# Attention, a feed-forward block and a gated convolution: both heads' scores of a pair from separate halves of the array

## The chip, the cores and the metric

The kernel runs on one core of one Trainium2 chip. The metric is the device time of one execution in microseconds; the time before is the median of three executions. Engines: TensorE (PE; its weight loads are shown apart as PEld), VectorE (DVE), ScalarE (ACT), GpSimd (POOL), SyncE (SP), from whose queue all loads and stores are issued.

## The reference, cut to what matters

```python
# q, k, v: (8, 8, 576, 64): 8 batches, 8 heads, 576 positions, 64 wide
scores = (q @ k.T) / 8.0
scores = where(row // 64 >= col // 64, scores, -1e9)       # causal by blocks of 64
attn = exp(scores - rowmax); attn = attn / (rowsum + 1e-9)
x = heads side by side of (attn @ v)                       # (8, 576, 512)
u = x + ((x.T @ U) @ V).T                                  # rank 32 over positions
u = u + relu(u @ w_ch1) @ w_ch2                            # 512 -> 2048 -> 512
gate = sigmoid(causal convolution of u with 5 taps, per channel)
out = (gate * (u @ w_val)) @ w_out
```

## The kernel before, in words

There are 64 heads, handled in pairs: queries and keys of a pair are loaded together as 128 rows (64 of each head) by 576 columns, and VectorE transposes them in 32 x 32 blocks (`prep_t`, lines 348 to 366). One call of `tick(n, ...)` (line 723) is one step of a software pipeline: it computes the scores of head n and, two heads behind, the product with v of head e = n - 2 (`emit_pv`), with the exponents of head e + 1 between them (`emit_est`); `mixing` puts in the rank-32 mixing of finished pairs. `tick` is a generator; each `yield` is a point at which other work may be put in.

Scores come in two forms. Heads 0 to 17 (n < NQ = 18) have queries on the rows: `emit_q_bank` (line 420) makes four PSUM banks of scores per head in plain float32, 1856 columns in all. Both heads' transposed queries are the stationary operand on all 128 rows, and the moving operand is a copy of the head's keys that holds zeros on the other head's 64 rows (the tiles ks and qs of the list kz, zeroed in `setup_att`). VectorE masks a block, takes the row maxima from PSUM and ScalarE writes the exponents from PSUM; TensorE transposes those later (`emit_q_turn`).

Heads 18 to 63 have keys on the rows: `emit_s_piece` (line 389) computes the scores in four pieces of 512, 320, 448 and 320 columns (1600 in all; the first is made of stretches of 64, 192 and 256), each in its own PSUM bank. The operands are rounded parts in the one-pass format float32r, made by `prep_qk` (line 368): ScalarE rounds q once and k twice (three casts of 64 x 576, helper line 93), GpSimd clears half of a tile (line 380) and subtracts for the two remainders kl and qs (helper line 99). Two 128-row matmuls per stretch of columns (lines 397 and 398) then give high by high plus high by low, and low by high. ScalarE copies each piece to a buffer (line 402), GpSimd sets the masked corners (`emit_corners`, line 475), VectorE finds the column maxima (`emit_max_a`, `emit_max_b` and `emit_max_c`, lines 488 to 522, with small copies between partitions at 508 to 518) and subtracts them (`emit_sub`, line 525, five instructions a head at line 528); ScalarE takes the exponents in place (line 550) and rounds them, VectorE takes the remainders el.

What sets the order. TensorE runs in the order in which the code is written. The other engines' instructions are ordered beforehand by a planner that works with the dependences and its own estimates, and each engine then runs its queue in that order. Up to about 127 us only attention runs (with the splitting of the feed-forward weights on ScalarE, VectorE and GpSimd). From then on the loop at line 1083 goes over 9 groups of 512 positions with 16 slices of the hidden layer each: `emit_h1` makes a slice (12 matmuls into a PSUM tile h, read by ScalarE as hh and by VectorE as the remainder hl, lines 869 and 870), `emit_o` adds the slice before it to four accumulators (12 matmuls, line 887). At four places of each slice `gap()` takes the next step or steps of the attention from `tick`, at a pace that `aim` sets so that a batch of eight heads is done when its group is due; what is not done by then is run off before the next group starts. In this stage the accumulators hold four of the eight PSUM banks, and score tiles, h, and all tiles of attention share the other four (the pool of `ps_p`, tag a). Before it the scores have four banks of their own. From about 1085 us only the feed-forward block is left, and from about 1325 us the gated stage.

Of the kernel before, what the change touches and what calls it, by code (L numbers as in the profile page):

```python
# [22 lines left out]
def attn_moe_gate_kernel(ctx: ExitStack, tc: tile.TileContext, q, k, v, U, V, w1, w2, wval, convw, wout, out):  # L23
# [35 lines left out]
    QV = 10  # L59
    KV = 0  # L60
# [138 lines left out]
    st_p = rpool("stp", 1)  # L199
    s_p = rpool("sp", 2)  # L200
# [103 lines left out]
    def setup_att():  # L304
        for t in vstk:
            pool.memset(t[:, :, D:P], 1.0)
            pool.memset(t[0:D, NK - 1, :], 0.0)
        for a in range(2):
            for t in kz:
                pool.memset(t[a][own[1 - a]], 0.0)  # L310
# [29 lines left out]
    def pads(nm, dtype):  # L340
        return [st_p.tile([P, S], dtype, tag=f"{nm}{a}", name=f"{nm}{a}") for a in range(2)]

    kz = [pads(nm, F32) for nm in ("ks", "qs")]
    ks, qs = [], []
    kl = st_p.tile([P, S], F32R, name="kl")
    qkt = {}

    def prep_t(pn):
        if pn >= B * NP:
            return  # L350
        t = raw.pop(pn)
        if 2 * pn < NQ:
            tq = rot("tk" if pn % 2 else "tq", 1)
            z = kz[pn % 2]
            for rows in own if pn == 0 else (slice(0, P),):
                vec.transpose(tq[rows], t["q"][rows])
                for a in range(2):
                    if pn or rows == own[a]:
                        vec.transpose(z[a][own[a]], t["k"][own[a]])
            qkt[pn] = (tq, z)  # L360
        else:
            tq, tk = rot("tq", 1), rot("tk", 1)
            vec.transpose(tq, t["q"])
            vec.transpose(tk, t["k"])
            qkt[pn] = (tq, tk)
        load_qk(pn + 1)

    def prep_qk(n):
        if n >= B * H or n < NQ:
            return  # L370
        if not ks:
            ks.extend(pads("ks", F32R))
            qs.extend(pads("qs", F32R))
        tq, tk = qkt[n // 2]
        a = n % 2
        me, ot = own[a], own[1 - a]
        hi_act(qs[a][me], tq[me])
        hi_act(ks[a][me], tk[me])
        hi_act(ks[a][ot], tk[me])
        pool.memset(f32(kl[ot]), 0.0)  # L380
        lo(vec if n < KV else pool, kl[me], tk[me], ks[a][me])
        lo(vec if n < QV else pool, qs[a][ot], tq[me], qs[a][me])

# [5 lines left out]
    def emit_s_piece(n, i):  # L389
        pr, a = divmod(n, 2)  # L390
# [781 lines left out]
```

## Time and profile before

| | |
|---|---|
| three executions | 1532.7 us median, 1532.04 to 1533.65 |
| the profiled execution | 1538.09 us, span in the profile 1536.3 us |
| TensorE busy | 1427.0 us, 93% of the span (weight loads 1151.1) |
| VectorE busy | 1146.3 us, 75% |
| ScalarE busy | 789.5 us, 51% |
| GpSimd busy | 516.1 us, 34% |
| DMA | 163.58 MB, 106 GB/s over the span |

A busy share is an average over stages with different limits, so the stretches have to be read by themselves. A matmul's recorded length includes its way through the array; how many follow each other in a time is read from their starts. One float32 matmul leaves two records (a weight load and a matmul each), a float32r matmul one. The granted clock is that of TensorE, 1.00 being 2.4 GHz; it has two levels, and the other is 1.2 GHz.

### The profile page before, as it was taken

Reading aid. Unit: us, or ns where it says so; the run is one execution under the profiler, and the core shown is the slowest. Engines: PE = TensorE matmul, PEld = TensorE weight load, DVE = VectorE, ACT = ScalarE, POOL = GpSimd, SP = SyncE. Lnnn points to the kernel's source line nnn. Section 1 sums busy time; section 2 is a strip of 40 time slices with the busy share of each in tenths; the row PEclk is TensorE's granted clock in tenths of the full one; section 3 lists DMA queues with packets and bytes.
Section 4 is the critical chain, followed back from the end, with each engine's and each line's share of the span. In section 5 each row is a group of like instructions: output and inputs, shape, how many; then the busy total and the mean of one; then the engine's idle time right before and its main releaser. Section 6 shows DMA issues by size and latency. Waiting matters only on the chain. (4 is left out here: it accounts for less than half of the span.)

```text
span 1536.3 us, 20391 instructions
## 1 busy us (share of the span) xinstructions
PE 1427.0 (93%) x6664; PEld 1151.1 (75%) x6664; DVE 1146.3 (75%) x2252; ACT 789.5 (51%) x1639; POOL 516.1 (34%) x587
## 2 busy tenths in 40 slices
PE   5897899979989998999899989989999999999999
PEld 2665677868767787777687778768888888778887
DVE  7887874659887888788888878887624427399991
ACT  4785565546565665666476556655512212243432
POOL 3133232333435333534443444335104210353410
PEclk8998999989999999999999999999999999999999
DMA  7555662224233333333323333232225543323221
GB/s 171 142 133 167 204 194 79 79 80 103 79 81 114 85 86 105 92 79 89 109 79 90 92 92 93 78 85 90 77 83 198 174 135 123 105 68 103 78 74 69
DMA packets 246291, 163.58 MB, mean 106 GB/s; under 512 B 197669, under 2 KB 212261, under 8 KB 246186
## 3 DMA queue, kind: packets, MB, share of 16 engines
q1 hardware_dynamic: 246186, 162.29, 36.6%
q8 instruction: 53, 0.87, 0.2%
q14 instruction: 52, 0.43, 0.1%
HBM read 134.98 MB, written 27.26 MB: 106 GB/s over the span
## 5 line engine op out<-in xcount | busy, mean ns | idle before, releaser
L887 PE MATMUL acc<-hh,w 128*128 128x512 f32 x1152 | 408.4, 405 | 10.2 <-ACT hh L869 10.2
L887 PEld LDWEIGHTS acc<-hh,w 128*128 128x128 f32 x1152 | 220.7, 192 | 57.7 <-ACT hh L869 12.8
L841 PE MATMUL h<-uh,w1hi 128*128 128x512 f32 x576 | 239.1, 415 | 9.9 <-DVE hl L870 6.3
L887 PE MATMUL acc<-hl,w 128*128 128x512 f32 x576 | 230.2, 400 | 5.9 <-DVE hl L870 5.9
L841 PE MATMUL h<-uh,w1lo 128*128 128x512 f32 x576 | 228.2, 396 | 0.0
L841 PE MATMUL h<-ul,w1hi 128*128 128x512 f32 x576 | 228.0, 396 | 0.0
L870 DVE SCALAR_TENSOR_TENSOR hl<-h,hh 128x512 fp32r<-128x512 f32 x144 | 98.2, 682 | 116.1 <-ACT hh L869 115.4
L869 ACT ACTIVATE hh<-h 128x512 fp32r<-128x512 f32 x144 | 85.8, 596 | 154.3 <-PE h L841 147.4
L550 ACT ACTIVATE s<-s 128x448 f32<-128x448 f32 x92 | 65.5, 712 | 150.0 <-DVE s L528 149.0
L841 PEld LDWEIGHTS h<-uh,w1hi 128*128 128x128 f32 x576 | 110.7, 192 | 35.8 <-DVE hl L870 8.2
L402 ACT COPY s<-pS 128x320 f32<-128x320 f32 (+2 forms) x184 | 89.8, 490 | 80.9 <-PE pS L398 77.2
L887 PEld LDWEIGHTS acc<-hl,w 128*128 128x128 f32 x576 | 110.5, 192 | 27.5 <-DVE hl L870 8.2
L841 PEld LDWEIGHTS h<-uh,w1lo 128*128 128x128 f32 x576 | 109.7, 190 | 24.8
L841 PEld LDWEIGHTS h<-ul,w1hi 128*128 128x128 f32 x576 | 110.7, 192 | 18.3 <-issue 1.4
L528 DVE TENSOR_TENSOR s<-s,mb 128x64 f32<-128x64 f32 (+4 forms) x230 | 123.0, 598 | 1.3
L962 DVE SCALAR_TENSOR_TENSOR gt<-yb,cw,gt 128x516 f32<-128x516 f32 (+1 forms) x144 | 116.5, 839 | 1.4
L99 POOL TENSOR_TENSOR vlo<-vstk,vhi 128x320 fp32r<-128x320 f32 x46 | 54.3, 1180 | 161.1 <-ACT vhi L93 148.1
L99 POOL TENSOR_TENSOR yl<-yb,yh 128x512 fp32r<-128x512 f32 (+7 forms) x64 | 67.7, 1091 | 96.9 <-ACT yh L93 96.8
L99 POOL TENSOR_TENSOR ul<-xt,uh 128x512 fp32r<-128x512 f32 (+7 forms) x64 | 53.2, 840 | 132.6 <-ACT uh L93 131.9
L397 PE MATMUL pS<-qs,ks 128*128 128x320 f32 (+4 forms) x276 | 80.4, 309 | 6.3 <-ACT lt L614 4.2
L398 PE MATMUL pS<-qs,kl 128*128 128x320 f32 (+4 forms) x276 | 82.4, 302 | 0.0
L99 DVE TENSOR_TENSOR el<-s,eh 128x448 fp32r<-128x448 f32 x92 | 76.7, 859 | 5.2 <-issue 4.6
(152 smaller groups left out, 3105.5 us busy)
## 6 DMA issues: line engine op xcount, KB each, us to landing
w<-w_s SPq DMA_DIRECT2D x144, 512.0 KB, 3.2
rawq<-in_q_dram SPq DMA_DIRECT2D x128, 72.0 KB, 2.4
rawk<-in_k_dram SPq DMA_DIRECT2D x128, 72.0 KB, 2.5
out_dram<-ot SPq DMA_DIRECT2D x35, 256.0 KB, 2.0
raw<-in_moe_w_ch_dram SPq DMA_DIRECT2D x64, 128.0 KB, 2.3
raw<-in_moe_w_ch_dram SPq DMA_DIRECT2D x16, 512.0 KB, 4.2
vstk<-in_v_dram SPq DMA_DIRECT2D x64, 128.0 KB, 2.6
w_s<-wo SPq DMA_DIRECT2D x16, 512.0 KB, 3.6
```

Of the source, the lines that this page charges most:

```text
L99: eng.tensor_tensor(o, i, f32(h), op=ALU.subtract)
L397: pe.matmul(ps[:, o:o + w], ks[a][:, kslice(j)], qs[a][:, a0:a1], start=True, stop=False)
L398: pe.matmul(ps[:, o:o + w], kl[:, kslice(j)], qs[a][:, a0:a1], start=False, stop=True)
L402: act.copy(stt[n][half_of[j]][:, d:d + o], ps[:, 0:o])
L528: noted(3, vec.tensor_tensor(sv(n, j), sv(n, j), mb[:, q0[j]:], op=ALU.subtract))
L550: act.activation(s, s, AF.Exp, scale=scale)
L841: pe.matmul(ps[:, 0:n], w[:, d, fs], x[:, d, 0:n], start=(d == 0 and i == 0), stop=(d == ND - 1 and i == 2))
L869: act.activation(hh[:, 0:n], ps[:, 0:n], AF.Relu)
L870: latest[0] = vec.scalar_tensor_tensor(hl[:, 0:n], ps[:, 0:n], 0.0, f32(hh[:, 0:n]), op0=ALU.max, op1=ALU.subtract)
L887: pe.matmul(acc[d][:, 0:n], w[:, wi, ds], x[:, 0:n], start=(f == 0 and i == 0), stop=(f == NF - 1 and i == 2))
L962: vec.scalar_tensor_tensor(gt[d][:, 0:gw], y[:, d, j:j + gw], cw[:, d, j:j + 1], gt[d][:, 0:gw], op0=ALU.mult, op1=ALU.add)
```

## The change

Scores are computed for both heads of a pair in the even head's `tick`. A new function, `beside`, takes two PSUM banks and issues for each stretch of columns one plain float32 matmul per head, with the transposed queries and keys of that head on their own 64 rows (0 to 63, 64 to 127), so that no zeros are needed. `prep_qk`, the rounded parts and the zeroed tiles go, and `prep_t` makes one transposed tile each of queries and keys. Both score forms use `beside`; an odd head's `tick` issues no scores, and its corners and first maxima move from its fourth step to its first. The score buffers go from two to three. For the first 18 heads the order of the banks changes: the small rest of the last query tile comes with the first bank, is copied out by ScalarE and its exponent is taken two instructions later, where before a bank was kept waiting for it.

```diff
--- before.py
+++ after.py
@@ -56,8 +56,6 @@
     ABUF = 4
     RAWB = 2
     WAB = 2
-    QV = 10
-    KV = 0
     UVE = 0
     HPOS = 8
     GPOS = 6
...
-    st_p = rpool("stp", 1)
-    s_p = rpool("sp", 2)
+    s_p = rpool("sp", 3)
...
-        for a in range(2):
-            for t in kz:
-                pool.memset(t[a][own[1 - a]], 0.0)
...
-    def pads(nm, dtype):
-        return [st_p.tile([P, S], dtype, tag=f"{nm}{a}", name=f"{nm}{a}") for a in range(2)]
-
-    kz = [pads(nm, F32) for nm in ("ks", "qs")]
-    ks, qs = [], []
-    kl = st_p.tile([P, S], F32R, name="kl")
...
     def prep_t(pn):
         if pn >= B * NP:
             return
         t = raw.pop(pn)
-        if 2 * pn < NQ:
-            tq = rot("tk" if pn % 2 else "tq", 1)
-            z = kz[pn % 2]
-            for rows in own if pn == 0 else (slice(0, P),):
-                vec.transpose(tq[rows], t["q"][rows])
-                for a in range(2):
-                    if pn or rows == own[a]:
-                        vec.transpose(z[a][own[a]], t["k"][own[a]])
-            qkt[pn] = (tq, z)
-        else:
-            tq, tk = rot("tq", 1), rot("tk", 1)
-            vec.transpose(tq, t["q"])
-            vec.transpose(tk, t["k"])
-            qkt[pn] = (tq, tk)
+        tq, tk = rot("tq", 1), rot("tk", 1)
+        for rows in own if pn == 0 else (slice(0, P),):
+            vec.transpose(tq[rows], t["q"][rows])
+            vec.transpose(tk[rows], t["k"][rows])
+        qkt[pn] = (tq, tk)
         load_qk(pn + 1)
-
-    def prep_qk(n):
-        if n >= B * H or n < NQ:
-            return
-        if not ks:
-            ks.extend(pads("ks", F32R))
-            qs.extend(pads("qs", F32R))
-        tq, tk = qkt[n // 2]
-        a = n % 2
-        me, ot = own[a], own[1 - a]
-        hi_act(qs[a][me], tq[me])
-        hi_act(ks[a][me], tk[me])
-        hi_act(ks[a][ot], tk[me])
-        pool.memset(f32(kl[ot]), 0.0)
-        lo(vec if n < KV else pool, kl[me], tk[me], ks[a][me])
-        lo(vec if n < QV else pool, qs[a][ot], tq[me], qs[a][me])

...
-    def emit_s_piece(n, i):
-        pr, a = divmod(n, 2)
+    def beside(pn, i, todo):
+
+        tq, tk = qkt[pn]
+        ps = [psum["a"].tile([P, 512], F32, tag="a", name="pS") for _ in own]
+        for q_, k_, o, by_key in todo:
+            w = (q_ if by_key else k_).stop - (q_ if by_key else k_).start
+            for a, me in enumerate(own):
+                l_, r_ = (tk[me, k_], tq[me, q_]) if by_key else (tq[me, q_], tk[me, k_])
+                pe.matmul(ps[a][:, o:o + w], l_, r_, start=True, stop=True)
+        return ps
+
+    def emit_s_piece(pn, i):
+        heads = (2 * pn, 2 * pn + 1)
         if i == 0:
-            stt[n] = [s_p.tile([P, w], F32, tag=f"s{h}", name=f"s{h}") for h, w in enumerate(sw)]
-        ps = psum["a"].tile([P, 512], F32, tag="a", name="pS")
-        o = 0
+            for n in heads:
+                stt[n] = [s_p.tile([P, w], F32, tag=f"s{h}", name=f"s{h}") for h, w in enumerate(sw)]
+        todo, o = [], 0
         for j, a0, a1 in pieces[i]:
-            w = a1 - a0
-            pe.matmul(ps[:, o:o + w], ks[a][:, kslice(j)], qs[a][:, a0:a1], start=True, stop=False)
-            pe.matmul(ps[:, o:o + w], kl[:, kslice(j)], qs[a][:, a0:a1], start=False, stop=True)
-            o += w
+            todo.append((slice(a0, a1), kslice(j), o, True))
+            o += a1 - a0
         j, a0, a1 = pieces[i][0]
         d = soff[j] + a0 - q0[j]
-        act.copy(stt[n][half_of[j]][:, d:d + o], ps[:, 0:o])
+        for n, ps in zip(heads, beside(pn, i, todo)):
+            act.copy(stt[n][half_of[j]][:, d:d + o], ps[:, 0:o])
...
     qbanks = [
+        [(2, 0, 3 * P, 0), (4, 4 * P, S, 3 * P)],
+        [(4, 0, 4 * P, 0)],
         [(3, 0, 4 * P, 0)],
-        [(4, 0, 4 * P, 0)],
-        [(2, 0, 3 * P, 0), (4, 4 * P, S, 3 * P)],
         [(0, 0, P, 0), (1, 0, 2 * P, P)],
...
-    def emit_q_bank(n, i):
-
-        a = n % 2
-        tq, z = qkt[n // 2]
...
-        r, nm, _ = qmax[n]
-        ps = psum["a"].tile([P, 512], F32, tag="a", name="pS") if i else _
-        for t, k0, k1, o in qbanks[i]:
-            pe.matmul(ps[:, o:o + k1 - k0], tq[:, kslice(t)], z[a][:, k0:k1], start=True, stop=True)
...
-        if i == 1:
-            eqs[n]["wait"] = ps
-            return
...
-        for t, k0, k1, o in qbanks[i] + (qbanks[1] if i == 2 else []):
-            src = eqs[n]["wait"] if i == 2 and t == NTT - 1 and k0 == 0 else ps
-            act.activation(eqs[n][t][:, k0:k1], src[:, o:o + k1 - k0], AF.Exp, bias=nm[:, t:t + 1], scale=scale)
+            for n in heads:
...
+                t = tiny_p.tile([P, 2 * NTT + 2], F32, tag="rq", name="rq")
+                qmax[n] = t[:, 0:NTT + 1], t[:, NTT + 1:]
+        todo = [(kslice(t), slice(k0, k1), o, False) for t, k0, k1, o in qbanks[i]]
+        for n, ps in zip(heads, beside(pn, i, todo)):
+            r, nm = qmax[n]
+            e = eqs[n]
+            if i == 0:
+                vec.memset(ps[0:D, 3 * P - D:3 * P], MASKED)
+            elif i == 2:
+                vec.memset(ps[0:D, 4 * P - D:4 * P], MASKED)
+            elif i == 3:
...
+            for t, k0, k1, o in qbanks[i]:
+                c = t + (k0 > 0)
+                vec.reduce_max(r[:, c:c + 1], ps[:, o:o + k1 - k0], axis=AX.X)
+            if i == 1:
+                x = vec.tensor_scalar(nm[:, 4:5], r[:, 4:5], r[:, 5:6], -scale, op0=ALU.max, op1=ALU.mult)
+            else:
+                c0, c1 = ((2, 3), None, (3, 4), (0, 2))[i]
+                x = vec.tensor_scalar(nm[:, c0:c1], r[:, c0:c1], -scale, None, op0=ALU.mult)
+            noted(1, x)
+            noted(3, x)
+            for t, k0, k1, o in qbanks[i]:
+                if k0:
+                    act.copy(e[t][:, k0:k1], ps[:, o:o + k1 - k0])
+                else:
+                    act.activation(e[t][:, k0:k1], ps[:, o:o + k1 - k0], AF.Exp, bias=nm[:, t:t + 1], scale=scale)
+            if i == 1:
+                act.activation(e[4][:, 4 * P:S], e[4][:, 4 * P:S], AF.Exp, bias=nm[:, 4:5], scale=scale)
...
         for i in range(4):
-            if n < NQ:
-                emit_q_bank(n, i)
-            elif new:
-                emit_s_piece(n, i)
-            if i == 3 and new and n >= NQ:
+            if new and n % 2 == 0:
+                (emit_q_bank if n < NQ else emit_s_piece)(n // 2, i)
+            if i == (0 if n % 2 else 3) and new and n >= NQ:
                 emit_corners(n)
                 emit_max_a(n)
             yield
@@ -741,7 +711,6 @@
                 emit_max_b(n)
             if n % 2 == 1:
                 prep_t((n + 1) // 2)
...
-    prep_qk(0)
```

## Rows read from the trace of the kernel before

**Rows 1.** Stretches: us, length, busy PE PEld DVE ACT POOL, clock, DMA, GB/s

```profile
...
43.00:127.00 84.00, 72.97 (x362) 49.63 (x362) 71.24 (x211) 64.39 (x156) 21.37 (x19) 0.96 0.53 138
...
176.00:308.00 132.00, 129.16 (x619) 99.55 (x617) 84.68 (x193) 75.11 (x161) 38.28 (x39) 1.00 0.43 124
...
1085.00:1325.00 240.00, 240.00 (x1085) 198.59 (x1084) 101.43 (x175) 60.53 (x118) 37.95 (x36) 1.00 0.39 133
...
266.00:1085.00 819.00, 759.70 (x3687) 628.65 (x3686) 681.22 (x1327) 486.77 (x992) 335.90 (x409) 0.97 0.33 89
...
```

**Rows 2.** TensorE's waits, 270 to 1090 us: total us, times, longest

```profile
...
PE pPV L612 <- DVE hl L870: 11.5, 5, 2.3
PE acc L887 <- ACT hh L869: 10.2, 6, 2.0
...
PE acc L887 <- DVE hl L870: 5.9, 6, 1.7
PE pS L397 <- ACT lt L614: 4.2, 10, 0.5
...
PE h L841 <- DVE hl L870: 3.2, 5, 0.6
...
PE pS L397 <- DVE x L99: 1.9, 4, 0.7
...
```

**Rows 3.** Timeline of TensorE, one head's four pieces: start us, us, work

```profile
...
507.48 0.30 PE L397 MATMUL pS<-qs,ks 128*128 128x64 f32 x1 [0.36 <-ACT lt L614]
...
508.27 0.40 PE L841 MATMUL h<-uh,w1hi 128*128 128x512 f32 x1
...
509.67 0.31 PE L397 MATMUL pS<-qs,ks 128*128 128x320 f32 x1
...
509.96 0.40 PE L887 MATMUL acc<-hh,w 128*128 128x512 f32 x1
...
```

**Rows 4.** Timeline of TensorE, one head of the float32 form

```profile
...
62.30 3.41 PE L432 MATMUL pS<-ks,tq 128*128 128x512 f32 x12
65.55 0.76 PE L612 MATMUL pPV<-e,vstk 128*128 128x128 f32 x3
...
```

**Rows 5.** Timeline, the only matmuls on fewer than 128 rows

```profile
...
1179.23 0.39 PE L887 MATMUL acc<-hh,w 128*128 128x512 f32 x1
1179.55 0.32 PEld L277 LDWEIGHTS pC<-unit,wa 5*128 5x128 f32 x4 [0.35 <-issue]
...
1180.23 0.40 PE L841 MATMUL h<-ul,w1hi 128*128 128x512 f32 x1
...
```

**Rows 6.** Groups of ScalarE and GpSimd, 266 to 1085 us

```profile
...
L93 ACT CAST ks<-tk 64x576 fp32r<-64x576 f32 x88 | 59.0, 671 | 8.4 <-PE pS L397 6.0 <-DVE tk L364 1.4
...
L93 ACT CAST qs<-tq 64x576 fp32r<-64x576 f32 x44 | 29.5, 671 | 0.5
...
L99 POOL TENSOR_TENSOR qs<-tq,qs 64x576 fp32r<-64x576 f32 x44 | 67.6, 1536 | 8.2 <-ACT qs L93 5.7
L99 POOL TENSOR_TENSOR kl<-tk,ks 64x576 fp32r<-64x576 f32 x45 | 64.4, 1431 | 3.1
...
```

**Rows 7.** Timeline, five subtractions of two heads, and GpSimd near them

```profile
...
754.01 2.10 DVE L528 TENSOR_TENSOR s<-s,mb 128x64 f32<-128x64 f32 x5
...
756.79 1.60 POOL L900 TENSOR_TENSOR y<-y,ul 128x512 f32<-128x512 f32 x1 [4.86 <-DVE y L899]
...
814.81 3.65 DVE L528 TENSOR_TENSOR s<-s,mb 128x64 f32<-128x64 f32 x5
...
815.48 1.42 POOL L99 TENSOR_TENSOR qs<-tq,qs 64x576 fp32r<-64x576 f32 x1
...
```

**Rows 8.** Timeline, one first-batch head; group of key transposes, 0 to 270 us

```profile
...
43.27 3.40 PE L432 MATMUL pS<-qs,tk 128*128 128x512 f32 x12
...
46.13 0.69 ACT L456 ACTIVATE s<-pS,rq 128x512 f32<-128x512 f32 x1 [1.22 <-DVE rq L443]
...
L359 DVE STREAM_TRANSPOSE ks<-rawk 64x576 f32<-64x576 f32 x10 | 7.7, 766 | 0.5 <-DMA rawk<-in_k_dram 0.2
...
```

More of the change, by code (lines that the diff above doesn't have):

```diff
@@ L418, in attn_moe_gate_kernel, with emit_q_bank @@
     qmax = {}
-    def emit_q_bank(n, i):
-        a = n % 2
-        tq, z = qkt[n // 2]
+    def emit_q_bank(pn, i):
+        heads = (2 * pn, 2 * pn + 1)
         if i == 0:
-            s0, s1 = (s_p.tile([P, w], F32, tag=f"s{h}", name=f"s{h}") for h, w in enumerate(sw))
-            eqs[n] = {3: s0[:, 0:4 * P], 1: s0[:, 4 * P:6 * P], 0: s1[:, 0:P], 2: s1[:, P:4 * P], 4: rot("m" if a else "mb", 1)}
-            t = tiny_p.tile([P, 2 * NTT + 2], F32, tag="rq", name="rq")
-            qmax[n] = (t[:, 0:NTT + 1], t[:, NTT + 1:], psum["a"].tile([P, 512], F32, tag="a", name="pS"))
-        r, nm, _ = qmax[n]
-        ps = psum["a"].tile([P, 512], F32, tag="a", name="pS") if i else _
-        for t, k0, k1, o in qbanks[i]:
-            pe.matmul(ps[:, o:o + k1 - k0], tq[:, kslice(t)], z[a][:, k0:k1], start=True, stop=True)
-        if i == 0:
-            vec.memset(ps[0:D, 4 * P - D:4 * P], MASKED)
-        elif i == 2:
-            vec.memset(ps[0:D, 3 * P - D:3 * P], MASKED)
-        elif i == 3:
-            vec.memset(ps.rearrange("p (c w) -> p c w", w=D)[0:D, 1:6:4, :], MASKED)
-        for t, k0, k1, o in qbanks[i]:
-            c = t + (k0 > 0)
-            vec.reduce_max(r[:, c:c + 1], ps[:, o:o + k1 - k0], axis=AX.X)
-        if i == 0:
-            x = vec.tensor_scalar(nm[:, 3:4], r[:, 3:4], -scale, None, op0=ALU.mult)
-        elif i == 2:
-            vec.tensor_tensor(r[:, 4:5], r[:, 4:5], r[:, 5:6], op=ALU.max)
-            x = vec.tensor_scalar(nm[:, 2:5:2], r[:, 2:5:2], -scale, None, op0=ALU.mult)
-        elif i == 3:
-            x = vec.tensor_scalar(nm[:, 0:2], r[:, 0:2], -scale, None, op0=ALU.mult)
-        if i == 1:
-            eqs[n]["wait"] = ps
-            return
-        noted(1, x)
-        noted(3, x)
-        for t, k0, k1, o in qbanks[i] + (qbanks[1] if i == 2 else []):
-            src = eqs[n]["wait"] if i == 2 and t == NTT - 1 and k0 == 0 else ps
-            act.activation(eqs[n][t][:, k0:k1], src[:, o:o + k1 - k0], AF.Exp, bias=nm[:, t:t + 1], scale=scale)
@@ new lines, in emit_q_bank @@
+            for n in heads:
+                s0, s1 = (s_p.tile([P, w], F32, tag=f"s{h}", name=f"s{h}") for h, w in enumerate(sw))
+                eqs[n] = {3: s0[:, 0:4 * P], 1: s0[:, 4 * P:6 * P], 0: s1[:, 0:P], 2: s1[:, P:4 * P], 4: rot(("m", "mb", "m2")[n % 3], 1)}
+                t = tiny_p.tile([P, 2 * NTT + 2], F32, tag="rq", name="rq")
[9 more added lines that the diff above has]
+            elif i == 3:
+                vec.memset(ps.rearrange("p (c w) -> p c w", w=D)[0:D, 1:6:4, :], MASKED)
+            for t, k0, k1, o in qbanks[i]:
[15 more added lines that the diff above has]
+                act.activation(e[4][:, 4 * P:S], e[4][:, 4 * P:S], AF.Exp, bias=nm[:, 4:5], scale=scale)
@@ L743, in tick @@
                 prep_t((n + 1) // 2)
-            prep_qk(n + 1)
         yield from mixing(2 * e, mixed, last)
```

## The prediction

> **What bounds it now.** The page's busy times (table above) name TensorE first; the stretches come next and say where it counts [rows 1]. From 1085 us to the end no scores are computed and TensorE has no gap until 1325 us, so nothing there can change. From 266 to 1085 us (main stage below) the feed-forward matmuls run with 46 heads of attention between them. TensorE is busy for 759.7 of 819 us, VectorE for 681, so TensorE is idle for 59 us, and its granted clock of 0.97 means that some 6% of the stage (0.03/0.5, 49 us) ran at 1.2 instead of 2.4 GHz, which cost up to 25 us more. From 43 to 127 us, in the attention of the first batch alone, TensorE has 73 and VectorE 71 of 84 us: two engines close to full. From 176 to 308 us it is TensorE again, 129 of 132.
>
> What ends TensorE's waits in the main stage [rows 2] is mostly VectorE's rounding remainder hl or a ScalarE result, a few us per batch of eight heads. So the change is worth what it does to TensorE's own time per pair, against what it takes out of these waits.
>
> **The change, part by part.**
>
> TensorE, main stage. Before, a head costs 0.79 us for the first piece (507.48 to 508.27), 0.29 for each 320-column piece, and 1.4 times that, 0.41, for 448 columns [rows 3]: 1.78 a head, 3.56 a pair. After, the matmuls are plain float32. Such a matmul is two records: twelve records over 1856 columns took 3.25 us from the first start to the next work's start [rows 4], or 0.876 ns per column of a record. A head has 1600 columns, 3200 record-columns, so the two heads take 5.61 us if nothing of them overlaps and 2.80 if all does. No row shows two matmuls on different rows of the array. What all rows show is that records start in the program's order; each head's second record has to wait for its own first, and the other head's first comes behind it. Then of four records two run together: three slots instead of four. By pieces: 1280 record-columns for the first (64, 192 and 256 columns chained), 960, 1344 and 960 for the rest, 4544 in all, 3.98 us. I take this, between the ends, since it follows from the order that the rows show.
>
> Going from 128 rows to 64 and back. The only matmuls with fewer rows are the four 5-row transposes at 1179.55 [rows 5]. From the last full matmul before them to the second after them 1.00 us passes; the two full ones take 0.23 each (six in the 1.40 us from 508.27 to 509.67 [rows 3]), and the four loads, 0.32 with the last one's own 0.14, stand 0.06 apart, so 0.24 for four. What is left, 0.30 us, is the price of going in and out. I take 0.30 per visit; the ends are 0 and 0.54 (all of the detour). Each of a pair's four steps stands between feed-forward matmuls [rows 3], so four visits, 1.20 us. The pair then costs 5.18 against 3.56: +1.62, times 23 pairs **+37 us**. The ends are 2.80 - 3.56 = -0.76 (-17 us) and 5.61 + 2.16 - 3.56 = +4.2 (+97).
>
> Removed in the main stage: per head three ScalarE casts (88.5 us in all), two GpSimd subtractions (132 us) and a memset [rows 6]. None is on TensorE's path by itself; what counts is who stood behind them. With GpSimd idle until 756.79 the five subtractions of a head took 2.10 us on VectorE; with the qs remainder at work beside them, 3.65 [rows 7]. ScalarE's exponent waits for these, and casts, evacuations and hh stand behind it in its queue. Of the waits in [rows 2], 36.9 us in all, I take away two thirds (1.55 us is two thirds of the longest kind there, 2.3): -25 us. Of the 25 us lost to the clock I take half, since the low stretches come with the waits: -13. **-38 us**; the ends are 0 and -62. The other waits (59 - 37) end on transposes and outputs that keep their producers.
>
> Added in the main stage: a step takes two of four PSUM banks at once. Behind a waiting score matmul stands everything that TensorE has to do. I cost it at nothing: the cover is the six feed-forward matmuls between two steps, 1.4 us [rows 3], against two copies of about 0.5 each. The odd head's copies, corner memsets and maxima move up by a tick, the corners past GpSimd's other work; that gives their readers more time. Loads on SP's queue keep number and place. The third score buffer keeps the same wait as before (a buffer of two heads back).
>
> First batches (nine float32 pairs). Before, a pair cost 6.50 us; after, with 4672 record-columns in three-slot order, 4.09 plus one or two visits, 4.5 where the steps stand together (six pairs) and 5.3 between feed-forward matmuls (three). Four of the six lie in the full stretch: 4 x 2.0 = 8 us. But the third step needs the banks of the first, and one head's first bank was read out by ScalarE only at 46.82, 3.55 us after its matmul began [rows 8], while two new steps take 2. So half goes back: **-4 us**. The other three save 1.2 each, half of that: **-2 us**. One transpose of 0.77 us [rows 8] goes for each of eight pairs, on VectorE; ScalarE gets a 64-column copy more per head. Both lie beside TensorE's work; uncovered they are -6 and at most +12 (18 times the 0.69 of the 512-column exponent there). The four memsets of the padding went ahead of a first matmul that anyway waits for a transposed q.
>
> **Sum:** 37 - 38 - 4 - 2 = -7 us. The profiled execution took 1538.1 us (span 1536.3), 5.4 above the median of 1532.7; carried over, 1531 there and 1526 beside the median. This case's own range is 1508 to 1545.
>
> **Rivals.**
>
> (1) Slower: the heads take turns. If the array doesn't run two halves together, a pair in the main stage costs 5.61 + 1.20 = 6.81, +3.25, +75 us; less 38 that is +37. The first stages gain nothing and pay some 7 us for their visits: +44, 1577. For it: every row shows one matmul after another. Against it: no row ever put two on separate rows. The point that decides is a pair at 5.2 us; above that the main stage loses. It is also the case in which the change doesn't do what it says. Chance 0.18.
>
> (2) The two heads overlap wholly: 2.80 + 1.20 = 4.00 a pair, 27 us less than forecast, and 3 less in the first stages, 1496. Visits at no price give nearly the same. For it: separate rows, separate banks. Against: program order. Chance 0.22. The Trainium skill, page "TensorE: Matmul & The Clock Gate", Part 3, says that matmuls on different row groups start about 4 ns apart, which would be this case; it measured one matmul per tile, not two records each, and no run here shows it.
>
> (3) The banks. If ScalarE is held up by an exponent, both banks of a step stay full, and each later step of a pair waits about one copy, 0.5 us: 23 x 3 x 0.5 = +35, 1561. For: ScalarE waits for VectorE often; against: the casts ahead of the copies are gone. Chance 0.10. The page "TensorEngine Tiling (Array Packing)", Restrictions and Gotchas, of the Trainium skill says that row tiling raises the pressure on PSUM; that speaks against this change, and by it this rival would be the likeliest.
>
> (4) The waits stay, since other work (the outputs' additions, the normalisation) sets them: relief 10 instead of 38, 1554. For: VectorE stays the second busiest engine. Against: the two rows of the five subtractions. Chance 0.08.
>
> **How the numbers follow.** The forecast has 0.42; with terms of both signs its own spread is about 18 us, so some 0.27 of it lies below -0.2% (3 us, about what a measurement can tell here), 0.05 within and 0.10 above. Rival 2 adds 0.21 to faster. Rivals 1, 3 and 4 add 0.33 to slower, with 0.02 each for same and for faster from their edges. Faster 0.50, same 0.07, slower 0.43. The range runs from rival 2 less some relief, 1490, to rival 1, 1577.
>
> **What would show it.** Right: two heads' records start in threes of slots, a pair's first step takes about 1.1 us and a 320-column step 0.85; about 0.15 us of TensorE gap on either side of it; no GpSimd beside the five subtractions and 2.1 us for them; TensorE idle in the main stage down from 59 to some 35 us. Wrong: records of the second head that start only after both of the first; score matmuls waiting for a ScalarE copy; waits in the main stage as long as before; a clock below 0.97 there.

## The result, and the profile after

The changed kernel takes 1552.5 us (median of four runs, 1547.9 to 1553.4) against 1533.2 for the kernel before in the same session: ratio 1.0116, 95% interval 1.0091 to 1.0142, some 19 us slower. The profiled execution took 1551.8 us, with a span of 1550.1. The forecast was 1526, faster. The time lies inside the whole range (1490 to 1577), but outside the range of the forecast's own case (1508 to 1545).

Where it went is read from four moments, the starts of feed-forward groups of 512 positions (the expectations below call a group a batch of the feed-forward). The first matmul of the first group starts at 127.5 us before and at 164.2 after: **+36.7**. The first group itself takes 187.4 before and 184.4 after. From the second group's start to the seventh's, five groups, it is 723.3 before and 699.6 after: **-23.7**. The seventh takes 115.7 and 120.7. From there on both are alike to 1.3 us. The spans of the two profiles differ by 13.8 us and not by 19, since the profiled execution before was 5.4 us above its median. So the change gains in the main stage and loses more than that before the feed-forward begins.

The first matmul of the feed-forward in the timeline of TensorE, before and after (start us, us, work):

```profile
127.53 0.78 PE L841 MATMUL h<-uh,w1hi 128*128 128x512 f32 x1
...
164.22 0.78 PE L810 MATMUL h<-uh,w1hi 128*128 128x512 f32 x1
```

Two stretches that answer to [rows 1], in the same columns:

```profile
43.00:127.00 84.00, 66.76 (x293) 43.39 (x292) 53.88 (x154) 50.97 (x124) 14.10 (x12) 0.82 0.51 115
...
266.00:1085.00 819.00, 780.15 (x3778) 595.76 (x3774) 626.69 (x1343) 416.63 (x886) 173.84 (x274) 0.98 0.36 92
```

From 266 to 1085 us TensorE's idle time fell from 59 to 39 us, VectorE's busy time from 681 to 627 and GpSimd's from 336 to 174 us. The changed kernel is some 35 us late when this window opens and over 10 us when it closes, so the same work is better compared, from the second group's start to the seventh's, before and after:

```profile
314.90:1038.20 723.30, 668.72 (x3243) 553.62 (x3242) 610.96 (x1183) 432.32 (x880) 295.89 (x361) 0.97 0.33 90
...
348.60:1048.30 699.70, 668.59 (x3243) 513.45 (x3242) 552.05 (x1181) 358.96 (x760) 148.47 (x241) 0.98 0.37 93
```

TensorE is busy for as long as before; its idle time fell from 54.6 to 31.1 us, and that is nearly the whole gain. From 43 to 127 us it is the other way round: TensorE 67 instead of 73 us, VectorE 54 instead of 71, and the granted clock 0.82 instead of 0.96. No engine is full there any more, and less gets done.

**The main stage, TensorE.** One pair's four steps in the timeline of TensorE (columns as in [rows 3], to which they answer):

```profile
409.89 0.39 PE L856 MATMUL acc<-hh,w 128*128 128x512 f32 x1
410.20 1.25 PE L360 MATMUL pS<-tq,tk 64*128 64x64 f32 x12
411.38 0.51 PE L856 MATMUL acc<-hh,w 128*128 128x512 f32 x1
...
412.67 0.39 PE L856 MATMUL acc<-hh,w 128*128 128x512 f32 x1
412.99 0.81 PE L360 MATMUL pS<-tq,tk 64*128 64x320 f32 x4
413.73 0.50 PE L810 MATMUL h<-uh,w1hi 128*128 128x512 f32 x1
...
414.99 0.40 PE L810 MATMUL h<-uh,w1lo 128*128 128x512 f32 x1
415.32 1.02 PE L360 MATMUL pS<-tq,tk 64*128 64x448 f32 x4
416.27 0.50 PE L810 MATMUL h<-uh,w1hi 128*128 128x512 f32 x1
...
417.52 0.39 PE L810 MATMUL h<-uh,w1lo 128*128 128x512 f32 x1
417.84 0.81 PE L360 MATMUL pS<-tq,tk 64*128 64x320 f32 x4
418.58 0.50 PE L856 MATMUL acc<-hh,w 128*128 128x512 f32 x1
```

From the start of the last full matmul ahead of a step to the start of the next one behind it: 1.49, 1.06, 1.28 and 1.06 us. Each holds one full matmul, 0.23, so the pair costs 4.89 - 0.92 = 3.97 us, against the 5.18 of the forecast and the 4.00 of its rival 2. The trace also shows the overlap record by record: in 57 of the 60 steps of 320 and 448 columns from the second group to the seventh, the four records start in two couples, 6 to 8 ns apart within a couple: one record of each head, since one head's two records start 0.37 us apart (experiment 6, 320 columns). And from 320 to 448 columns a pair's step grows by 0.22 us, which is 256 record-columns at 0.876 ns [rows 4], those of one head alone.

The 3.56 before is a little high. Its 0.79 for the first piece [rows 3] was read right behind a wait of 0.36 us; that price stands in 10 of the 40 heads of these five groups, and most take 0.68, as here:

```profile
731.15 0.19 PE L397 MATMUL pS<-qs,ks 128*128 128x64 f32 x1
...
731.83 0.39 PE L841 MATMUL h<-uh,w1hi 128*128 128x512 f32 x1
```

The mean of the 40 is 0.71, so a pair cost 3.40 by the same sum, and it costs 0.57 more now.

**The main stage, waits.** The view that answers to [rows 2] (total us, times, longest):

```profile
PE pT L652 <- DVE xt L685: 28.8, 5, 5.9
PE pT L644 <- DVE xt L685: 8.0, 1, 8.0
PE h L810 <- ACT s L426: 0.5, 1, 0.5
```

The many short waits for hl, hh and lt are gone. In their place another one has grown, about once a group, to 5.9 us: the transpose of xt at a group's boundary. In the same view before it stands with 14.8 us in all, here with 36.8:

```profile
PE pT L680 <- DVE xt L713: 8.4, 5, 3.1
PE pT L672 <- DVE xt L713: 6.4, 1, 6.4
```

The group of VectorE's subtractions over the whole span (total us, mean ns), which answers to [rows 7], before and after:

```profile
L528 DVE TENSOR_TENSOR s<-s,mb 128x64 f32<-128x64 f32 (+4 forms) x230 | 123.0, 598 | 1.3
...
L500 DVE TENSOR_TENSOR s<-s,mb 128x64 f32<-128x64 f32 (+4 forms) x230 | 105.6, 522 | 0.4
```

A head's five take 5 x 522 = 2.6 us on the mean; before it was 5 x 598 = 3.0 us. The 2.1 that the prediction looked for is the best case, not the mean.

**Before the feed-forward.** One pair's scores in the first form, all engines (start us, us, engine, work, in brackets the idle time before it and what ended it):

```profile
106.97 2.00 PE L360 MATMUL pS<-tk,tq 64*128 64x384 f32 x12
...
108.31 1.15 DVE L97 TENSOR_TENSOR g<-t,g 32x128 fp32r<-32x128 f32 x1
109.49 0.69 DVE L414 TENSOR_REDUCE rq<-pS 128x1 f32<-128x384 f32 x2
...
110.51 0.58 ACT L426 ACTIVATE s<-pS,rq 128x384 f32<-128x384 f32 x1 [2.23 <-DVE rq L419]
...
111.24 1.12 PE L360 MATMUL pS<-tk,tq 64*128 64x512 f32 x2 [2.27 <-ACT m L424]
...
113.00 3.04 PE L360 MATMUL pS<-tk,tq 64*128 64x512 f32 x10 [0.64 <-DVE pS L409]
...
115.98 5.19 PE L584 MATMUL pPV<-e,vstk 128*128 128x128 f32 x12
...
124.79 2.98 PE L584 MATMUL pPV<-e,vstk 128*128 128x128 f32 x12
```

The first two steps go into all four banks in 2.0 us. The third has to wait until ScalarE has read the first bank, 4.3 us after that was begun (106.97 to 111.24); its second head and the fourth step stand behind it. The product with v that comes next takes 5.19 us where twelve such matmuls take 2.98 at 124.79: it runs at 1.2 GHz for most of its length, after the waits, and the granted clock of this tick is 0.75 (next view). The stretches of the same pair, the tick with its scores and the tick without, in the columns of [rows 1]:

```profile
107.00:120.50 13.50, 10.59 (x36) 6.15 (x36) 12.14 (x37) 6.87 (x20) 1.40 (x1) 0.75 0.23 58
120.50:134.30 13.80, 10.74 (x56) 8.03 (x54) 6.66 (x13) 9.88 (x23) 5.16 (x5) 0.88 0.49 94
```

And two heads of the kernel before, which has scores in each tick:

```profile
80.70:99.50 18.80, 17.58 (x87) 11.94 (x87) 15.80 (x48) 14.82 (x38) 5.43 (x5) 1.00 0.60 159
```

In the changed kernel VectorE is busy for 12.1 of 13.5 us in the one tick and 6.7 of 13.8 in the other; the pair takes 27.3 us where two heads took 18.8.

### The profile page after: what moved, and what is told of

Read it like the earlier page. It is cut to its first block, busy times and chain, and to the rows that moved or that the text cites. A ratio compares the mean times of both kernels' runs of the same rounds, so it can differ in the third digit from the quotient of the medians.

```text
span 1550.1 us, 20078 instructions
## 1 busy us (share of the span) xinstructions
PE 1441.3 (93%) x6664; PEld 1106.5 (71%) x6664; DVE 1081.7 (70%) x2244; ACT 710.2 (46%) x1519; POOL 347.7 (22%) x445
## 4 chain that ended last, share of the span: by engine, by line
PE 77%; DVE 13%; DMA 5%; ACT 2%; issue 2%; SPq 1%; POOL 1%; DVEq 0%; ACTq 0%
PE h L810 23%; PE acc L856 23%; PE pPV L584 9%; PE pS L360 7%; PE o L973 7%; PE val L949 5%; DMA raw<-in_moe_w_ch_dram 4%; DVE rq L414 1%; DVE s L500 1%; PE pG L660 1%; DVE y L868 1%; DVE wa L125 1%; PE pT L644 1%; DVE el L97 1%; DVE m L464 1%
## 5 line engine op out<-in xcount | busy, mean ns | idle before, releaser
L856 PE MATMUL acc<-hh,w 128*128 128x512 f32 x1152 | 402.1, 404 | 0.0
L810 PEld LDWEIGHTS h<-uh,w1hi 128*128 128x128 f32 x576 | 111.0, 193 | 49.0 <-issue 21.7
L97 POOL TENSOR_TENSOR vlo<-vstk,vhi 128x320 fp32r<-128x320 f32 x46 | 42.8, 930 | 372.9 <-ACT vhi L91 354.1
L856 PEld LDWEIGHTS acc<-hl,w 128*128 128x128 f32 x576 | 110.1, 191 | 19.3 <-DVE hl L839 0.5
L375 ACT COPY s<-pS 128x320 f32<-128x320 f32 (+2 forms) x184 | 81.8, 496 | 75.2 <-PE pS L360 73.6
L500 DVE TENSOR_TENSOR s<-s,mb 128x64 f32<-128x64 f32 (+4 forms) x230 | 105.6, 522 | 0.4
L360 PE MATMUL pS<-tq,tk 64*128 64x320 f32 (+4 forms) x552 | 90.8, 428 | 0.0
L97 DVE TENSOR_TENSOR el<-s,eh 128x448 fp32r<-128x448 f32 x92 | 70.7, 800 | 22.8 <-PE pPV L584 18.2
L360 PE MATMUL pS<-tk,tq 64*128 64x512 f32 (+4 forms) x216 | 60.6, 585 | 26.6 <-ACT m L424 8.1
## 6 DMA issues: line engine op xcount, KB each, us to landing
raw<-in_moe_w_ch_dram SPq DMA_DIRECT2D x64, 128.0 KB, 2.3
vstk<-in_v_dram SPq DMA_DIRECT2D x64, 128.0 KB, 2.8
```

Of the source, the lines that this page charges most:

```text
L97: eng.tensor_tensor(o, i, f32(h), op=ALU.subtract)
L360: pe.matmul(ps[a][:, o:o + w], l_, r_, start=True, stop=True)
L375: act.copy(stt[n][half_of[j]][:, d:d + o], ps[:, 0:o])
L500: noted(3, vec.tensor_tensor(sv(n, j), sv(n, j), mb[:, q0[j]:], op=ALU.subtract))
L810: pe.matmul(ps[:, 0:n], w[:, d, fs], x[:, d, 0:n], start=(d == 0 and i == 0), stop=(d == ND - 1 and i == 2))
L856: pe.matmul(acc[d][:, 0:n], w[:, wi, ds], x[:, 0:n], start=(f == 0 and i == 0), stop=(f == NF - 1 and i == 2))
```

## The experiments

Line numbers are those of each kernel. "Start" is the first feed-forward matmul. Ratios are to the kernel before in the same session.

**1. Only the main stage with both heads at once.** The first nine pairs use the functions of the kernel before (`emit_q_bank`, its order of banks, `prep_t` with padded keys; the padded keys of odd pairs lie in one of the three score buffers). Against the changed kernel:

```diff
-            if new and n % 2 == 0:
-                (emit_q_bank if n < NQ else emit_s_piece)(n // 2, i)
+            if n < NQ:
+                emit_q_bank(n, i)
+            elif new and n % 2 == 0:
+                emit_s_piece(n // 2, i)
```

> The first nine pairs as before (one head at a time, keys padded with zeros to 128 rows, the old order of the four steps), the main stage with both heads of a pair at once. Theory 'the loss lies in the first form': the feed-forward starts at about 127.5 us as before instead of 164.2, and the batches behind it keep what the change gained there (3 us up to the second batch, 23.6 us from the second to the seventh, 4.9 us lost in the eighth): about 1511 us, 1505 to 1518. Rival 'the first batch is late for another reason' (fewer casts shift the order of the instructions, the loads of the weights): the feed-forward starts near 164 again and the run takes 1545 or more.

Measured: 1517.0 us, ratio 0.9910 (0.9882 to 0.9938). Start at 128.0; from the second group to the seventh 699.6. The stretch up to the start:

```profile
0.00:128.00 128.00, 97.46 (x438) 64.66 (x439) 103.21 (x292) 83.81 (x197) 33.83 (x43) 0.92 0.60 146
```

So the loss lies in the first form, the gain in the main stage, and this version beats both kernels.

**2. The reverse.** The first form as changed, the main stage with `prep_qk`, `emit_s_piece` and the rounded parts of before.

```diff
-            if new and n % 2 == 0:
-                (emit_q_bank if n < NQ else emit_s_piece)(n // 2, i)
+            if n < NQ and n % 2 == 0:
+                emit_q_bank(n // 2, i)
+            elif new and n >= NQ:
+                emit_s_piece(n, i)
```

> The reverse: the first nine pairs with both heads at once, the main stage with rounded parts and one head at a time as before. If the two parts add up: the feed-forward starts at about 164 us, and the whole takes 1532.7 + 36.7 = about 1569 us (1558 to 1575). If the gain of the main stage hangs on a late first batch (work that moved behind it), the sum of this kernel's and the other half's difference to before misses +19 us by more than 6.

Measured: 1564.4 us, ratio 1.0222 (1.0185 to 1.0259), start at 159.8. The two halves are worth +34 and -13 us, together +20.5; the whole change measured +19.3. They add up within the 6 us of the expectation, though this start lies 4.4 us ahead of the changed kernel's.

**3. First form, one head at a time on its 64 rows.**

```diff
-    def emit_q_bank(pn, i):
+    def emit_q_bank(n, i):
-        heads = (2 * pn, 2 * pn + 1)
+        heads = (n,)
...
-        for n, ps in zip(heads, beside(pn, i, todo)):
+        for n, ps in zip(heads, beside(n // 2, i, todo, (n % 2,))):
```

> As the changed kernel, but in the first form the four steps are issued for one head at a time, each in its own 64 rows (no padded keys, the new order of the steps, Exp copies and three buffers kept). Theory 'a pair at once takes two of the four banks a step, so steps 3 and 4 wait for VectorE and ScalarE, TensorE idles and its clock falls': the start of the feed-forward comes back to 125 to 135 us and the run to 1508 to 1520. Rival 'the 64-row float32 form itself, or the switch in and out of it, is what holds the clock at the lower level': it stays at 155 to 170 us and 1543 to 1556, the granted clock of 43 to 127 us stays near 0.82.

Measured: 1525.9 us, ratio 0.9968 (0.9950 to 0.9986), start at 136.4; the granted clock of 43 to 127 us is 0.91. The stretch up to the start, then the same of the changed kernel and of the kernel before:

```profile
0.00:136.40 136.40, 111.80 (x438) 70.20 (x439) 99.03 (x283) 86.78 (x209) 32.69 (x40) 0.89 0.56 137
```

```profile
0.00:164.20 164.20, 114.37 (x450) 71.06 (x451) 111.55 (x305) 93.05 (x218) 35.89 (x41) 0.82 0.54 126
```

```profile
0.00:127.50 127.50, 95.42 (x438) 63.13 (x439) 105.01 (x292) 83.74 (x196) 34.26 (x44) 0.93 0.59 147
```

Of the 36.7 us, 28 come back although 64-row matmuls of one head cost TensorE more than those of a pair. The time misses the theory's range by 6 us and the start by 1.4: the form itself, with what came with it (the order of the banks, one more ScalarE copy, single transposed tiles), keeps 8 or 9 us.

**4. Two steps in each tick.** Still both heads at once.

```diff
-            if new and n % 2 == 0:
-                (emit_q_bank if n < NQ else emit_s_piece)(n // 2, i)
+            if n < NQ and i % 2 == 0:
+                emit_q_bank(n // 2, n % 2 * 2 + i // 2)
+            elif new and n >= NQ and n % 2 == 0:
+                emit_s_piece(n // 2, i)
```

> As the changed kernel, but a pair's four steps in the first form are issued two in the even tick and two in the odd one, each still for both heads at once, with other work of the tick between. Theory 'banks': half of the burst is gone, the feed-forward starts at 130 to 150 us and the run takes 1515 to 1538. Rival 'form or switch': as the changed kernel, 1545 to 1556. Rival 'the next pair's transposes into single buffers wait for the last score': worse than the changed kernel, since the last step comes a tick later, over 1556.

Measured: 1531.9 us, ratio 1.0002 (0.9990 to 1.0014), start at 142.5. As the first theory expected, spreading the same work, with the same banks a step, gives back 22 of the 36.7 us.

**5. More banks.** Steps 3 and 4 of a pair take banks of the other pool.

```diff
-        ps = [psum["a"].tile([P, 512], F32, tag="a", name="pS") for _ in own]
+        from_ = psum["a"] if i < 2 else ps_p
+        ps = [from_.tile([P, 512], F32, tag="a", name="pS") for _ in own]
```

> As the changed kernel, but in the first form steps 3 and 4 of a pair take their banks from the other pool (four banks, shared with the transposed exponents and the products with v), so that no step waits for the banks of steps 1 and 2. Theory 'the wait for banks costs the time': the waits of score matmuls for a ScalarE result go, the feed-forward starts at 128 to 145 us instead of 164 and the run takes 1515 to 1533. Rival 'the burst itself' (whatever its banks, the readers of eight banks in a row are late for the next work, and TensorE waits there instead): the wait moves to the transposes of the exponents or to the products with v, the start stays above 155 us and the run above 1543.

Measured: 1545.0 us, ratio 1.0062 (1.0042 to 1.0081), start at 153.8. A pair's four steps now take 3.1 us from the start of the first record to that of the last, where they took 7.5 to 8.5 (the third pair to the sixth). TensorE's waits up to the start (columns as above):

```profile
PE pPV L585 <- ACT s L427: 28.6, 6, 8.7
PE pE L445 <- ACT s L427: 12.1, 2, 7.6
```

The rival holds in its mechanism: the wait moves from the scores to the products with v, which use the same pool. Its bound of 155 us for the start is missed by 1.2. Four more banks give 10 us back; most of the loss stayed.

**6. The main stage with one head at a time on 64 rows**, otherwise experiment 1.

```diff
-    def emit_s_piece(pn, i):
-        heads = (2 * pn, 2 * pn + 1)
+    def emit_s_piece(n, i):
+        heads = (n,)
```

> As the first experiment (1517 us), but in the main stage too each head's steps are issued alone, in its own 64 rows and float32. By the rows a pair's record-columns take 2.80 us if two heads overlap wholly and 5.61 if nothing overlaps. Theory 'the heads overlap wholly in the changed kernel': 23 pairs lose 2.8 us each, and up to 1.2 more for four further visits to 64 rows: +64 to +92, 1581 to 1609 us. Three slots of four: +1.6 to +2.8 a pair, 1554 to 1581. Rival 'nothing overlaps and the visits are free': at most four visits more, 1517 to 1545.

Measured: 1585.4 us, ratio 1.0323 (1.0304 to 1.0342): the first theory's range. By the ratios it is 63 us above experiment 1, at the lower edge of that theory, so the time alone would not decide; the steps do. A single head's step of 320 columns in the timeline of TensorE:

```profile
348.06 0.39 PE L830 MATMUL h<-uh,w1lo 128*128 128x512 f32 x1
348.37 0.80 PE L377 MATMUL pS<-tq,tk 64*128 64x320 f32 x2
349.11 0.50 PE L830 MATMUL h<-uh,w1hi 128*128 128x512 f32 x1
```

It takes 1.05 us from full matmul to full matmul; the pair's took 1.06. For 448 columns it is 1.27 against 1.28. So the second head costs nothing: the two overlap wholly. Of the 1.05, 0.23 is the full matmul and 0.56 are 640 record-columns at 0.876 ns [rows 4], which leaves 0.26 for going to 64 rows and back; the forecast took 0.30.

**7. Both heads in the even tick, but one behind the other**, one bank a step, otherwise experiment 3.

```diff
-            if n < NQ:
-                emit_q_bank(n, i)
+            if n < NQ and n % 2 == 0:
+                emit_q_bank(n + i // 2, i % 2 * 2)
+                emit_q_bank(n + i // 2, i % 2 * 2 + 1)
```

> As the third experiment (single heads in 64 rows, 1526 us), but both heads' four steps are issued in the even tick, one head behind the other, one bank a step, nothing in the odd tick. Theory 'two banks at once': a step needs one bank only, so the feed-forward starts at 130 to 145 us and the run takes 1520 to 1535. Rival 'the burst': eight banks in a row through four, no work of the odd tick between, so the feed-forward starts at 155 us or later and the run takes 1543 or more.

Measured: 1546.2 us, ratio 1.0068 (1.0046 to 1.0090), start at 148.9. Nothing but the tick of the odd head's scores differs from experiment 3, and it costs 12.5 us up to the start and about 1% (15 us) in all. The time is the rival's; the start lies between the two.

**8 and 9. Work put back into the main stage of experiment 1**, with results that nothing reads: on GpSimd the memset and the two subtractions per head, on ScalarE the three casts.

```diff
+        pool.memset(x[ot], 0.0)
+        pool.tensor_tensor(x[me], tk[me], y[me], op=ALU.subtract)
+        pool.tensor_tensor(x[ot], tq[me], y[me], op=ALU.subtract)
```

```diff
+        hi_act(x.bitcast(F32R)[me], tq[me])
+        hi_act(y.bitcast(F32R)[me], tk[me])
+        hi_act(y.bitcast(F32R)[ot], tk[me])
```

> As the first experiment (1517 us), but in the main stage GpSimd again does two subtractions of 64 x 576 and the memset per head at the old places; their results are read by nothing. Theory 'the main stage gained by what left GpSimd': VectorE's five subtractions run beside them again and take up to 3.65 instead of 2.10 us, the exponents come late, and 8 to 18 us come back: 1525 to 1535. Rival 'the gain lies elsewhere' (casts of ScalarE, or the order of the steps): under 4 us, 1514 to 1521.

> As the first experiment, but in the main stage ScalarE again does three casts of 64 x 576 per head at the old places; their results are read by nothing. Theory 'the main stage gained by what left ScalarE': evacuations, hh and exponents stand behind the casts again, 8 to 18 us come back: 1525 to 1535. Rival: under 4 us, 1514 to 1521. If this and the run before both stay under 4 us, the gain comes from the score matmuls no longer waiting for casts and remainders.

Measured: GpSimd's work put back 1585.1 us, ratio 1.0319 (1.0300 to 1.0339); ScalarE's put back 1511.4, ratio 0.9841 (0.9823 to 0.9859). Neither expectation foresaw how far apart they are: against experiment 1 the one costs 63 us by the ratios, the other nothing. VectorE's groups from 610 to 890 us (total us, mean ns of one), first with GpSimd's work back, then experiment 1:

```profile
L492 DVE TENSOR_TENSOR m<-m,s 128x320 f32<-128x320 f32 (+2 forms) x44 | 33.5, 761 | 0.8
L528 DVE TENSOR_TENSOR s<-s,mb 128x64 f32<-128x64 f32 (+4 forms) x70 | 33.0, 534 | 0.1
L490 DVE TENSOR_TENSOR m<-s,s 128x448 f32<-128x448 f32 x15 | 22.4, 1497 | 0.0
```

```profile
L517 DVE TENSOR_TENSOR s<-s,mb 128x64 f32<-128x64 f32 (+4 forms) x80 | 35.5, 508 | 0.1
L481 DVE TENSOR_TENSOR m<-m,s 128x320 f32<-128x320 f32 (+2 forms) x48 | 22.8, 475 | 0.9
L479 DVE TENSOR_TENSOR m<-s,s 128x448 f32<-128x448 f32 x16 | 9.6, 601 | 0.0
```

The work stands at the old place, but the scores come earlier now, so it falls beside all of VectorE's 448-column maxima and no longer beside its subtractions. The 448-column maximum goes from 601 to 1497 ns (15 x 0.9 = 13 us in this stretch, which is two groups long), the other maxima from 475 to 761 (44 x 0.29 = 13 us). A group then takes 151.1 us where it took 139.5. So GpSimd's work can cost far more than the forecast allowed it, depending on what it falls beside, and ScalarE's casts, as work, cost nothing. That the ninth is even faster than the first comes from two groups (135.3 and 134.8 us instead of 140.2 and 139.9) in which the wait at the boundary is 2.0 and 2.1 us instead of 5.9; a group that has it in full still takes 139.7.

**10. The kernel before, profiled once more.**

> The kernel before, profiled once more, to see how far one profiled execution stands from another: the feed-forward starts within 2 us of 127.5, and the stretch from the second to the seventh batch takes 723 us within 8. If that stretch is 715 or less, the gain of 23.6 us there was partly the profiled execution's own slowness.

Measured: 1535.3 us, start at 127.3, 719.3 from the second group to the seventh. So the -23.7 above is good to about 4 us.

**11. Filling TensorE's wait.**

```diff
+        if i == 1:
+            tq, tk = qkt[pn]
+            for x in range(9):
+                for n, me in zip(heads, own):
+                    pe.matmul(eqs[n]["spare"][:, 3 * P + D:4 * P], tq[me, 0:P], tk[me, 0:D], start=True, stop=True)
```

> As the changed kernel, but after the second step of each pair in the first form TensorE gets 18 more small matmuls (64 rows, 64 columns, into unused columns of the first step's banks, nobody reads them), some 2 us of work where it waits 2 to 3 us for the banks of steps 3 and 4. Theory 'the fallen clock is a large part of the loss': the granted clock of 43 to 127 us rises from 0.82 to 0.9 or more, the feed-forward starts 6 to 15 us earlier than 164 and the run takes 1537 to 1547. Rival 'the wait itself is the loss': the clock may rise, but the start stays within 4 us of 164 and the run at 1548 to 1557.

Measured: 1601.6 us, ratio 1.0430 (1.0407 to 1.0453), start at 192.3. The filling didn't fill: it writes into a bank with pending readers and waited for them itself, then ran for 3.9 us:

```profile
131.63 0.43 PE L408 MATMUL pS<-tk,tq 64*128 64x64 f32 x2 [2.27 <-ACT m L432]
134.20 3.88 PE L408 MATMUL pS<-tk,tq 64*128 64x64 f32 x33 [2.14 <-ACT m L432]
```

On the clock it says nothing. On the path it does: from first to last start the scores of the six pairs ahead of the feed-forward span 82.1 us in all instead of 56.4, 25.7 more, and the start moved by 28. Nothing hides this time.

**12. The addition at the boundary earlier**, otherwise experiment 1.

```diff
-        if tick_count[0] % EVERY == 0:
+        if tick_count[0] % EVERY == 1:
```

> As the first experiment (1517 us), but the held-back additions of the main stage are issued in the odd ticks instead of the even ones, so that at a batch's boundary VectorE adds xt ahead of a head's five subtractions and not behind them. In the first experiment TensorE waits there once a batch 5.9 us for that addition (its result sits in the bank that the next transpose needs), and a 6.8 us stretch at half clock follows. Theory 'this one wait for a bank eats what is left of the relief': it goes in most batches, each of them 4 to 5 us shorter, 1488 to 1503 us. Rival 'it only moves' (another addition comes behind the next head's subtractions, or TensorE waits for something else at once): 1510 to 1521.

Measured: 1520.8 us, ratio 0.9911 (0.9894 to 0.9929), as experiment 1. TensorE's waits from 330 to 1050 us, first experiment 1, then this one:

```profile
PE pT L669 <- DVE xt L702: 28.8, 5, 5.9
```

```profile
PE pT L669 <- DVE hl L858: 26.3, 5, 7.2
```

The rival holds. The wait changes its name, not its length: what TensorE needs from VectorE there stands behind a head's subtractions and remainders either way.

## Why the prediction was wrong

**TensorE in the main stage, +37: mis-sized.** The failing step is "three slots instead of four". It was drawn from the order of the records: the second head's first record was taken to come behind the first head's second one. The trace shows the two first records 6 to 8 ns apart, and experiment 6 shows that a second head on the other half of the rows costs 0.01 us a step. The pair costs 3.97 and not 5.18, +0.57 over before, so 23 pairs cost +13. That is the price of rival 2. The Trainium skill, page "TensorE: Matmul & The Clock Gate", Part 3, had said that matmuls on different row groups start some 4 ns apart. The 6 to 8 ns here agree, for float32 matmuls of two records each. The price of a visit held (0.30 foretold; 0.26 in experiment 6), and so did TensorE's idle time from 266 to 1085 us (35 foretold, 39 measured).

**Waits and clock, -38: right in size, in good part by luck.** Over the five groups the time fell by 19.7 to 23.7 us (against the two profiles of before) with 20 pairs at +0.57, that is +11: a relief of 31 to 35, or 36 to 40 for 23 pairs. It is nearly all idle time; the clock, which was to give 13 of the 38, rose only from 0.97 to 0.98. The cause was GpSimd's work beside VectorE, but the subtractions that the prediction read from [rows 7] gave the smaller part. Of the 59 us by which VectorE's busy time fell over the five groups they gave 17: before, the 576-column subtraction took 1.98 us beside the qs remainder and 0.75 alone, but it stood beside it in 14 of 40 heads only. Another 29 came from one small copy between partitions (total us, mean ns, before and after):

```profile
L516 DVE COPY r<-r 32x18 f32<-32x18 f32 x40 | 36.9, 922 | 1.3
...
L488 DVE COPY r<-r 32x18 f32<-32x18 f32 x40 | 7.8, 196 | 1.3
```

Before, 20 of these 40 stood beside GpSimd's addition to xt and took 1.72 us on the mean; the others took 0.17. That addition is still there; it only falls elsewhere now. So this part of the gain came from the new order of the work, which the prediction did not foresee, and no run tested it alone. ScalarE's casts, as work, were no cause, as experiment 9 shows; what the waiting for their results had cost was not tested, but in the view of [rows 2] score matmuls waited for 6.1 us in all. The prediction left "transposes and outputs that keep their producers" as they were; the transpose of xt grew by 22 us. The Trainium skill, page "SBUF — State Buffer", section "SBUF: two separate sides", says that a GpSimd operation that reads SBUF and a VectorE operation with two inputs from SBUF lock each other out for a whole instruction. Experiment 8 agrees: the 448-column maximum gained 0.9 us beside subtractions of 1.4 to 1.6 us.

**First batches, -4 and -2: wrong in sign, and this decided.** Measured: +36.7 up to the start, -3 after it. The failing step is "half goes back because the third step needs the banks of the first". The row was the right one (3.55 us from matmul to read-out in [rows 8], 4.3 here), but the step was counted as TensorE's work less one short wait. The starts of five kernels take it apart: 128.0 (experiment 1, the form of before), 136.4 (3: one bank a step, both ticks), 142.5 (4: two banks a step, both ticks), 148.9 (7: one bank a step, one tick) and 164.2 (the changed kernel: two banks a step, one tick). The form with one head costs 8.4 us. Both heads in one tick cost 12.5 with one bank a step and 21.7 with two; two banks a step instead of one cost 6.1 over both ticks and 15.3 in one. So the two don't simply add: some 9 us come only where they meet. (The kernels that keep the first form of before start between 126.2 and 130.2 us, so some 2 us of each figure may lie in the order of the other engines' work.) Four more banks give 10.4 back (experiment 5); to which of the two these belong, no run shows. The tick was not in the prediction at all: it said "two engines close to full" of this stretch and then didn't ask what happens when VectorE's and ScalarE's reading of two heads falls into one tick. In the pair shown VectorE fills that tick, TensorE waits, and in the next tick VectorE is half idle.

By the stretches under experiment 3, TensorE is idle up to the start for 164.2 - 114.4 = 49.8 us instead of 127.5 - 95.4 = 32.1, +17.7, and busy for 19.0 us more, at a granted clock of 0.82 instead of 0.93. Most of this second part is the clock's: in the stretches up to the start in which the granted clock was 1.2 GHz, TensorE was busy for 45.5 of 57.6 us, before for 8.8 of 16.9. If all work takes twice its time there, the 36.7 us by which that busy time grew are an estimated 18 us lost; the twelve products with v above, 5.19 us against 2.98, took 1.7 times. Whether the clock would have stayed up with work in the waits, no run shows: experiment 11 was to tell and did not.

**Rival 3, the banks,** named the right shortage in the wrong stage. In the main stage, where six feed-forward matmuls stand between two steps, the view of waits has no score matmul that waited for a copy. In the first form nothing stands between them.

**Open.** The seventh group takes 4.9 us more than before; it does so in experiment 1 too (120.7 us), so it belongs to the main stage, and it wasn't looked into. Nor were the 8.4 us of the form taken apart into the visits to 64 rows, the order of the banks, the further copy and the single transposed tiles.

## What to carry to other kernels

Issuing two steps of a software pipeline at once saves time on the engine that issues them and crowds the engines that read the results: before doing it, sum each reader's work by tick, not by stage, and count the banks that lie between. Where two engines are near full, as in the first stage here, an even spread was worth more than the saving; where other work stands between the steps, as in the main stage, a pair's step cost no more than one head's and no score step waited. When work is taken from GpSimd, look for which VectorE instructions it ran beside: that, and not its own duration, is what it was worth.

## What was not expected of the hardware

Float32 matmuls of two heads on the two halves of the rows overlap wholly: 1.06 us for a pair's step against 1.05 for one head's. And 3.6 us of GpSimd work per head (1.63, 1.43 and 0.57) cost a group of eight heads 11.6 us, through VectorE's maxima, while three ScalarE casts of 0.67 us per head cost nothing. A VectorE copy of 0.17 us took 1.72 us on the mean where it stood beside a GpSimd addition of 1.43.
